# Chunk-selected attention with a gated feed-forward: the order of all work drawn anew, without a dependence of the weight transfers on the first loads

## The chip, the cores and the metric

The kernel runs on one core of one Trainium2 chip. The metric is device microseconds of the whole execution; lower is better. The core has five engines with a queue of instructions each, worked off in order: TensorE (PE), VectorE (DVE), ScalarE (ACT), GpSimd (POOL) and SyncE (SP). Transfers are issued by SyncE (all loads of q, k and v, the stores, and transposing copies inside the chip) and by GpSimd (the weights, which are turned from 32 to 16 bits on the way).

## The reference

```
k_min, k_max = min, max of k over chunks of 32 keys
ub  = sum_d max(q*k_min, q*k_max)          # a bound for each query and chunk, causal chunks only
sel = the 6 chunks with the largest ub, for each query
scores = q k^T / 8, kept where sel and causal; attn = softmax(scores); a = attn v
x   = a with the heads side by side         # 4*768 = 3072 rows of 8*64 = 512
out = (sigmoid(x w_gate) * (x w_val)) w_out # 512 -> 1536 -> 512
```

q, k and v have 4 batches, 8 heads, 768 positions and 64 columns; everything comes and goes in 32 bits.

## The kernel before

The 24 blocks of 128 queries are grouped in eight units of three blocks. Unit 0 holds the first blocks of batches 0, 1 and 2, where no choice of chunks is needed; its short way is the function `first` (names with `f`: `scf`, `expf`, `cmf`, `pvf`, `xf`, `xpsf`, `xTf`, with the batch as the number). Units 1 and 2 hold the rest of batch 0 (and the first block of batch 3); units 3 to 7 the rest of batches 1 to 3.

A unit goes through these steps. q and k are turned so that the head's columns lie across the partitions (`qn`/`kn` copy, `qT`/`kT` turn on TensorE, `qf`, `kt`, `hk`, `hq` copy back; from unit 3 on VectorE turns them itself: `k16`, `kt`, `qf0`). `kx0`, `kx1`, `kcr` take the chunks' minima and ranges, `qm` the positive part of q, `ub` the bounds on TensorE, and `ubn`, `mx`, `ap`, `apt`, `hqm` the choice, which is added to the scores as extra rows of the product. `sc` are the scores, `exp` the exponentials, `cm` the causal edge, `pv` the product with the values (`v16`), `rz` and `x` the division, `xps`/`xT` the turn back (from unit 3 on a transposing transfer on SyncE). Then the feed-forward: `g` and `v` are the gate's and the value's product for one of twelve blocks of 128 columns (`v_u0_2`: unit 0, block 2; `vb`, `gb` the third block of rows of the first four), `tanh` the gate, `hg` their product, `o0` to `o2` the output's product, `osb` and `out` the copy and the store. Units 4 with 5 and 6 with 7 share a faster product (`P`, `E`, `C`, `S`, `T`, `Q`, `F`, `G`).

Loads: `k0_u1` to `q3_u2` bring a pair of heads' k or q for unit 1 (192 KB) or unit 2 (128 KB); `kf0_1`, `qf1_2` and the like bring half the heads of a batch's first block (128 KB); `vf_1` brings that block's values (256 KB); `v_0_3` the values of a later block; `k01_3` and the like a quarter of a batch's k (384 KB). There are 31 loads ahead of the first `v_0_*`. The weights come in nine pieces, `wg0` to `wg2`, `wv0` to `wv2`, `wo0` to `wo2`; pieces 0 serve the blocks 0 to 3 of the feed-forward, pieces 1 the blocks 4 to 7, pieces 2 the blocks 8 to 11.

Nothing chooses at run time. Each step is an `Op` with its reads, writes and possible engines; `ORDER` is a written-out list of all of them, with the engine where it is not the first possible one (`@DVE`) and the numbers of the buffers that are taken (`:5,0,1`). `Plan.order` reads it, and the instructions are issued to their engines in this order. Semaphores follow from reads and writes of data; the dependences that `Op` records beyond that serve whoever draws up the list.

The weights' functions are these; `after` is a copy of one element of a loaded tile:

```python
def after(key, part, prio):
    plan.add(f"after{prio}", {POOL: (110, 150)}, lambda e: nc.gpsimd.tensor_copy(word[0:1, prio:prio + 1], ...),
             reads=[key], writes=[f"after{prio}"], prio=-2.0)

def weights(i, prio, after):
    lo, hi = 512 * i, 512 * i + 512
    return plan.add(f"wg{i}", {POOL: (760, 760)}, lambda e: nc.gpsimd.dma_start(wg16[:, :, lo:hi], wgs[:, :, lo:hi]),
             reads=after, writes=[("wg", i)], prio=prio, ...
```

`after0` to `after3` read the tiles of unit 1's q loads, `after4` to `after6` those of `vf_0`, `vf_1` and `vf_2`. `beat0`, `beat1`, ... are fillers: `BEATS[i]` turns of the unit matrix on TensorE whose result nobody reads. In the order before, GpSimd has these instructions ahead of the feed-forward's start:

```
ident epat v11 after3 tri hkq001 qn_u2_3 qn_u1_0 after0 hkq000 hkq100 hk1_u1_1 after1 hq0_u1_1 vf1_1 hq0_u1_3 v10 after4
hkq101 after2 vf1_3 hkf1 after6 vf1_2 after5 wv0 hk0_u1_2 wg0 wg1 wv1 wg2 hk1_u1_2 wv2 hq1_u1_2 hq1_u1_1 kn_u2_0 wo0
```

Of the kernel before, what the change touches and what calls it, by code (L numbers as in the profile page):

```python
# [97 lines left out]
ident q3_u1:0 epat0:0 k0_u1 tri0 ap1 epat q2_u1 k1_u1 q3_u2:1 q1_u1 q0_u1 kn_u1_0:0 qn_u1_3@DVE:1 ap0 v11 kf1_0:0
after3 beat0:7 kT_u1_0:0 tri kcr0 k3_u1 hkq011 qn_u1_2@DVE:2 kf0_0 hkq001@POOL hq0 kt_u1_0:0 qT_u1_2:1 qf1_0:1
hkp001@ACT hk0_u1_0 k2_u1 kx0_u1_0 qn_u2_3@POOL:0 qf0_0 kn_u1_1@DVE:2 hkp011@ACT qn_u1_1@DVE:3 vf_0:2 beat1:7  # L100
qT_u1_1:2 qn_u1_0@POOL:4 kT_u1_1:3 hk1_u1_0@ACT after0 hkq000@POOL qT_u1_0:4 kx0_u1_1 hkq100@POOL kn_u1_3:4 kf0_1:3
kx1_u1_0:0 kt_u1_1:0 beat2:7 kT_u1_3:5 kx1_u1_1 kfT_0:0 hk1_u1_1@POOL qf_u1_1@DVE:0 q0_u2 kt_u1_3:1 qT_u2_3:3 after1
qT_u1_3:6 kxf1:1 kf1_1 hk1_u1_3@ACT hq0_u1_1@POOL k2_u2 qf_u1_2 vf1_1:1 kn_u1_2@DVE:0 beat3:7 qfT_0:2 qf_u1_3 qf0_1:0
kxf0 kT_u1_2:1 hq0_u1_3@POOL qf1_1 qf16_0:4 v10 qm_u1_2@ACT:0 vf_1:0 hk0_u1_1 qf_u1_0 after4 qf_u2_3@DVE:1 kf16_0:0
kcr_f kx0_u1_3 hkq101@POOL vf_2:1 beat4:7 scf_0:0,4,1 after2 vf1_3:2 kfT_1:3 expf_0_1:2 kn_u2_2@DVE:4 expf_0_0 hkf1
kx0_u1_2 beat5:7 kT_u2_2:4 qf0_2:3 kx1_u1_3 kf16_1:3 q2_u2 ident16 qm_u1_3@ACT beat6:7 qfT_1:0 cmf_0_0@DVE qf1_2
v16_0_0@ACT cmf_0_1@DVE kx1_u1_2 qf16_1:4 kf1_2:0 beat7:7 pvf_0_0:3 hq0_u1_0 rzf_0_0:0 k1_u2 beat8:7 scf_1:0,5,1
xf_0_0:0 kx1_u2_2:1 kf0_2 expf_1_0 xpsf_0_0:3,0 kt_u1_2@DVE:0 k3_u2 after6 expf_1_1:3 vf1_2:3 hk0_u1_3 k0_u2
qm_u1_0@ACT after5 vc_1@DVE wv0 qm_u1_1@ACT kx0_u2_2 q1_u2 hq1_u2_3 hk0_u1_2@POOL v_0_3:2 hkf0@ACT beat9:7 qfT_2:5 wg0
cmf_1_0@DVE pvf_0_1:1 v_0_2:1 xTf_0_0@ACT qn_u2_2@DVE:0 qf16_2@DVE:4 kn_u2_1:5 wg1 beat10:7 qT_u2_2:3 pvf_1_0:0  # L110
cmf_1_1@DVE beat11:7 kfT_2:5 kcr_u1 wv1 rzf_1_0:0 xf_1_0:0 kf16_2:0 rzf_0_1:1 wg2 hkq010 kn_u2_3:6 xf_0_1:1 beat12:7
scf_2:5,0,1 pvf_1_1:2 hk1_u1_2@POOL ub_u1:1,6 expf_2_1:2 rzf_1_1:1 wv2 xf_1_1:2 expf_2_0 cmf_2_1@DVE vc_2@ACT
cmf_2_0@DVE xpsf_1_1:5 xpsf_1_0:2 kT_u2_1:0 hq1_u1_2@POOL ubn1_u1:0 qf_u2_2 pvf_2_0:7 v_0_1:0 qm_u2_2@ACT:0 xpsf_0_1:3
hq1_u1_1@POOL rzf_2_0:1 pvf_2_1:6 xTf_1_0@ACT kx0_u2_1 kt_u2_2:0 kn_u2_0@POOL:3 xf_2_0:1 beat13:2 kT_u2_3:2 qn_u2_1:5
rzf_2_1:0 wo0 xTf_1_1@ACT xpsf_2_0:7 xf_2_1:0 kt_u2_1:1 qn_u2_0@DVE:6 beat14:4 xpsf_2_1:6 xTf_0_1@ACT ubn0_u1
qT_u2_1:5 hq0_u1_2@POOL xTf_2_0@ACT qT_u2_0:4 kx0_u2_3 xTf_2_1@ACT v_u0_2:1 hkp111@POOL kx1_u2_3 hkp000@ACT vb_u0_2
kt_u2_3@DVE:2 v_u0_1:6 ubm0_u1 mx0_u1:0 hk0_u2_3@POOL vb_u0_1 hkp010@ACT v_u0_0:2 wo1 vb_u0_0 ap0_u1 v_u0_3:7
qm_u2_3@POOL apt0_u1:0 qf_u2_0 vb_u0_3 kx1_u2_1 qf_u2_1 hqm0_u1_0@ACT ubm1_u1 hkp100 beat15:3 g_u0_0:0,0,0 mx1_u1
hk1_u2_3@POOL gb_u0_0 hk0_u2_1@POOL g_u0_3:5,1,1 hqm0_u1_2 tanh_u0_0 gb_u0_3 k00_1:1 sc_u1_0_2:4,0 hg_u0_0 sc_u1_0_1:0
wo2 tanh_u0_3 g_u0_1:3,2,2 exp_u1_0_1 gb_u0_1 hg_u0_3 g_u0_2:5,0,3 qm_u2_0@ACT hk0_u2_2 tanh_u0_1 gb_u0_2 qm_u2_1  # L120
sc_u1_1_0:7,2 hq0_u2_2@POOL exp_u1_0_2 hg_u0_1 sc_u1_0_0:3 exp_u1_1_0 hq0_u2_1@POOL sc_u1_1_2:0 sc_u1_2_2:4,1
g_u0_6:2,1,4 hkq111 tanh_u0_2 ap1_u1 exp_u1_1_2 sc_u1_2_1:7 hq1_u2_1@POOL g_u0_7:5,2,5 exp_u1_0_0 exp_u1_2_1 kT_u2_0:0
sc_u1_3_1:3,3 tanh_u0_7 g_u0_5:6,3,6 kx0_u2_0 tanh_u0_6 kx1_u2_0 sc_u1_2_0:5 hq1_u1_3@DVE tanh_u0_5 kcr_u2@POOL
kt_u2_0@DVE:2 exp_u1_3_1 v16_0_3@DVE hq1 apt1_u1 hg_u0_2 g_u0_4:7,0,7 sc_u1_3_2:6 v_u0_6:0 v_u0_7:3 hqm1_u1_0 v_u0_4:2
tanh_u0_4 hg_u0_7 hq1_u1_0@POOL exp_u1_2_2 v_u0_5:7 exp_u1_2_0 hg_u0_4 hq1_u2_2 ub_u2:4,3 cm_u1_2@DVE exp_u1_3_2
hg_u0_5 hkq110@ACT sc_u1_3_0:7 ubn1_u2:0 g_u0_10:6,3,8 exp_u1_3_0 hqm1_u1_2@DVE g_u0_11:3,0,9 hg_u0_6 ubn0_u2
g_u0_8:0,1,10 mx0_u2:0 sc_u1_1_1:4 g_u0_9:7,2,11 exp_u1_1_1 ap0_u2 v16_0_2@DVE v_u0_8:4 tanh_u0_9 kcr1 apt0_u2:0
tanh_u0_10 v_u0_11:7 cm_u1_3@DVE hqm0_u2_2@ACT cm_u1_0@DVE v_u0_10:6 tanh_u0_8 v16_0_1 v_u0_9:2 tanh_u0_11 hg_u0_10
hk1_u2_2@POOL hqm0_u2_0@ACT pv_u1_2:3 hg_u0_11 cm_u1_1 sc_u1_5_0:6,1 sc_u1_5_2:7 hg_u0_9 pv_u1_3 exp_u1_5_0 pv_u1_1:0
hg_u0_8 sc_u1_5_1:2 sc_u1_6_2:6,3 cm_u1_5 rz_u1_1:0 pv_u1_0 x_u1_1:0 exp_u1_6_2 sc_u1_6_0:4 hq0_u2_0@POOL o0_u0_0:5,1  # L130
exp_u1_5_1 exp_u1_6_0 sc_u1_4_2:2,0 sc_u1_6_1:3 cm_u1_6@DVE k01_1 sc_u1_7_1:4,2 exp_u1_4_2 sc_u1_7_0:6 rz_u1_0:0
sc_u1_4_0:1 x_u1_0:1 o0_u0_1:2,0 exp_u1_7_0 exp_u1_7_1 cm_u1_7@DVE o1_u0_1 exp_u1_5_2 mx1_u2 hk0_u2_0@ACT exp_u1_6_1
ap1_u2 sc_u1_4_1:7 sc_u1_7_2:4 o1_u0_0 apt1_u2 exp_u1_4_1 hqm1_u2_0@DVE exp_u1_7_2 exp_u1_4_0 xps_u1_1:7,0 pv_u1_5:4
xT_u1_1 pv_u1_7:3 hq1_u2_0 hqm1_u2_2@DVE pv_u1_6 sc_u2_1_0:7,2 hkp110 sc_u2_1_1:1 sc_u2_7_0:6,3 cm_u1_4 rz_u1_3:0
k10_1 sc_u2_7_2:0 x_u1_3:0 o2_u0_0 exp_u2_7_0 hk1_u2_1@POOL hkp101@POOL exp_u2_1_0 sc_u2_0_0:6,1 exp_u2_7_2
sc_u2_0_1:3 osb_u0_0@DVE pv_u1_4 exp_u2_0_0 hk1_u2_0@POOL xps_u1_3:0 sc_u2_6_1:5,0 rz_u1_2:0 k11_1 xps_u1_0:7
exp_u2_0_1 x_u1_2:0 o2_u0_1 xT_u1_0 xT_u1_3 sc_u2_7_1:7 sc_u2_6_0:0 osb_u0_1@DVE xps_u1_2:3 exp_u2_7_1 xT_u1_2
exp_u2_6_0 qf1_3:0 exp_u2_6_1 out_u0_0 o0_u0_2:4,1 sc_u2_1_2:3 o1_u0_2 hq0_u2_3 v_0_4:1 exp_u2_1_1 o2_u0_2 v_0_5:2
k16_1_2@ACT:3 k16_1_1@DVE:6 k16_1_0:5 g_u1_4:1,1,4 kx1_1_2:1 v_1_1:3 exp_u2_1_2 g_u1_0:5,2,8 cm_u2_1 cm_u2_0 osb_u0_2
kt_1_0:1 v_u1_3:3 cm_u2_7 q11_1:0 sc_u2_6_2:4 g_u1_3:0,0,9 kx0_1_1 hk0_1_0 exp_u2_6_2 v_u1_4:7 tanh_u1_3 kx1_1_3  # L140
cm_u2_6 tanh_u1_0 v_u1_2:4 v16_0_4 tanh_u1_4 kt_1_1:5 k16_1_3:0 sc_u2_0_2:5 v16_0_5@ACT v_u1_0:0 v_u1_7:1 hk0_1_1@ACT
kf1_3:2 hg_u1_0 out_u0_1 pv_u2_6:2 hg_u1_4 sc_u2_4_0:0,0 qf0_3 kx0_1_0 pv_u2_7 exp_u2_4_0 sc_u2_2_0:7,3 kf0_3
g_u1_2:6,1,10 exp_u2_0_2 rz_u2_3:0 q01_1 x_u2_3:0 v16_1_1@ACT v_u1_9:0 cm_u2_4@DVE kx1_1_0 tanh_u1_2 xps_u2_3:2,1
g_u1_7:5,2,11 exp_u2_2_0 kx0_1_2 xT_u2_3@ACT g_u1_9:6,3,5 tanh_u1_7 pv_u2_1:2 q00_1 hg_u1_7 tanh_u1_9 sc_u2_2_2:5
g_u1_11:7,2,6 hg_u1_2 hg_u1_3 sc_u2_3_2:4,2 v_u1_11:6 exp_u2_3_2 kx1_1_1 tanh_u1_11 qfT_3:3 q10_1 sc_u2_3_0:4 hg_u1_11
sc_u2_4_2:7 g_u1_10:1,0,7 hg_u1_9 v_u1_10:6 kt_1_3:6 tanh_u1_10 exp_u2_3_0 sc_u2_2_1:0 vf_3:0 pv_u2_0 hg_u1_10
exp_u2_2_1 g_u1_8:1,3,0 cm_u2_3 kx0_1_3 exp_u2_2_2 cm_u2_2 sc_u2_4_1:0 kfT_3:6 tanh_u1_8 rz_u2_0:0 k01_2:1 kcr_1@POOL
kt_1_2:0 qf16_3:4 sc_u2_5_0:5,1 v_u1_1:1 exp_u2_4_1 x_u2_0:0 g_u1_5:3,0,1 exp_u2_5_0 qf0_u3_0:1 kf16_3:3 sc_u2_5_1:2
hk1_1_0@DVE sc_u2_3_1:5 k11_2 v_u1_5:0 vc_3 qf0_u3_1 exp_u2_3_1 qf0_u3_2 sc_u2_5_2:6 exp_u2_4_2 v_u1_6:5 qf0_u3_3
exp_u2_5_1 xps_u2_0:7 cm_u2_5@DVE v_u1_8:4 tanh_u1_5 qm_u3_0@POOL:0 qf0_u4_2:0 k00_2 qm_u3_2@ACT hg_u1_5 pv_u2_3:3  # L150
pv_u2_2 exp_u2_5_2 xT_u2_0 qf0_u4_1 g_u1_6:7,0,2 hg_u1_8 hk1_1_1 scf_3:6,0,3 rz_u2_1:0 pv_u2_4:4 x_u2_1:0 expf_3_0
k10_2 pv_u2_5 g_u1_1:3,3,3 expf_3_1:0 cmf_3_0@DVE rz_u2_2:0 ub_u3:6,2 cmf_3_1 qf0_u4_3 tanh_u1_1 x_u2_2:1 tanh_u1_6
hq1_u3_0@POOL hg_u1_1 hk1_1_3@ACT v_1_2:0 hg_u1_6 pvf_3_1:7 pvf_3_0:1 hk1_1_2 xps_u2_1:4 o0_u1_0:3,0 rzf_3_1:0
out_u0_2 xf_3_1:0 rzf_3_0:1 hk0_1_2 v_2_1:2 ubn0_u3:0 o1_u1_0 qf0_u4_0 ubm0_u3 k16_2_0@ACT:0 xf_3_0:2 k16_2_3:2
q01_2:0 o2_u1_0 xT_u2_1 mx0_u3:0 k16_2_2@ACT:5 hq0_u3_2@POOL xpsf_3_1:4 o0_u1_1:1,1 ubn1_u3 ap0_u3 xps_u2_2:2 ubm1_u3
# [1253 lines left out]
```

## Time and profile before

| | us |
|---|---|
| median of 3 runs | 282.54 (280.86 to 287.28) |
| profiled execution, its own time | 282.25 |
| its span, first to last instruction | 280.2 |
| TensorE busy | 268.8 (96%) |
| VectorE busy | 246.8 (88%) |
| ScalarE busy | 220.4 (79%) |
| GpSimd busy | 134.6 (48%) |
| read from memory, written | 30.67 MB, 6.29 MB |

A row of a group gives busy time and the mean of one instruction; a row in order of time gives the start, the duration and, in brackets, the idle time ahead of it with what ended it. In a table by stage the columns are the stretch, its length, busy time with the count for PE, PEld (the weights' load into the array), DVE, ACT and POOL, then the granted clock, the busy share of the DMA engines and GB/s. L968 is the line of `g` and `v`, L876 of `sc`, L480 of the fillers, L359, L361 and L365 of copies on ScalarE, VectorE and GpSimd, L528, L529 and L534 of the weights, L936 of the transposing transfer, L573 of the quarters of k and q, L583 of `v_*`.

### The profile page before, as it was taken

How to read it: one execution, taken by the hardware profiler on the slowest of the kernel's cores; microseconds unless marked ns; L12 is line 12 of the kernel's file. 1: busy time of each engine (PE TensorE's matmuls, PEld its weight loads, DVE VectorE, ACT ScalarE, POOL GpSimd, SP SyncE). 2: the span in 40 equal slices, each digit the busy share in tenths (PEclk: the TensorE clock that was granted, in tenths of full speed). 3: DMA queues.
4: the chain of work that ended last, by engine and by line, in shares of the span. 5: the costliest groups of instructions: out<-in, count | busy, mean ns of one | idle time of the engine just before them, and what ended most of it. 6: DMA issues, size and time to landing. Idle time of an engine off the chain costs nothing.

```text
span 280.2 us, 7449 instructions
## 1 busy us (share of the span) xinstructions
PE 268.8 (96%) x2758; PEld 186.3 (67%) x2758; DVE 246.8 (88%) x679; ACT 220.4 (79%) x474; POOL 134.6 (48%) x206
## 2 busy tenths in 40 slices
...
GB/s 187 261 225 186 197 195 205 165 186 159 209 167 201 203 214 167 140 196 169 214 170 155 27 14 45 91 1 54 0 18 44 0 100 82 2 37 0 4 37 225
DMA packets 131699, 34.68 MB, mean 124 GB/s; under 512 B 119760, under 2 KB 128720, under 8 KB 131664
## 3 DMA queue, kind: packets, MB, share of 16 engines
...
q0 software_dynamic: 4752, 4.72, 10.2%
...
HBM read 30.67 MB, written 6.29 MB: 132 GB/s over the span
## 4 chain that ended last, share of the span: by engine, by line
PE 83%; DVE 5%; ACT 4%; DMA 3%; issue 2%; SPq 1%; POOL 0%; ACTq 0%; DVEq 0%
PE sc_u L876 12%; PE g_u L968 11%; PE v_u L968 10%; PE o_u L1006 10%; PE pv_u L912 6%; PE suo_u6u L1233 3%; PE suo_u4u L1233 3%; PE sug_u4u L1092 3%; PE suv_u4u L1092 3%; PE sug_u6u L1092 2%; PE suv_u6u L1092 2%; PE ube_u L814 2%; DMA k<-in_k_dram 2%; DMA kq_u<-in_q_dram 1%; PE sro_u4u L1233 1%
## 5 line engine op out<-in xcount | busy, mean ns | idle before, releaser
L887 ACT ACTIVATE att_u<-sc_u 128x512 f16<-128x512 f32 (+3 forms) x184 | 90.9, 549 | 15.1 <-PE sc_u L876 12.7
L896 POOL TENSOR_SCALAR_AFFINE_SELECT att_u<-att_u 128x384 f16<-128x384 f16 (+1 forms) x48 | 26.8, 570 | 44.0 <-ACT att_u L887 42.8
L968 PE MATMUL g_u<-xT_u,wg 128*128 128x384 f16 (+2 forms) x208 | 37.6, 314 | 0.0
L968 PE MATMUL v_u<-xT_u,wv 128*128 128x384 f16 (+2 forms) x208 | 36.4, 313 | 0.0
L1006 PE MATMUL o_u<-wo,hg_u 128*128 128x512 f16 x144 | 35.3, 379 | 0.1
L876 PE MATMUL sc_u<-hqe,hke 128*128 128x128 f16 (+2 forms) x220 | 28.2, 243 | 1.6 <-ACT hqe L359 1.2
L987 DVE SCALAR_TENSOR_TENSOR hg_u<-gate_u,v_u 128x384 f16<-128x384 f16 x48 | 24.8, 538 | 4.7 <-PE v_u L968 3.1
L912 PEld LDWEIGHTS <-att_u 128*128 128x128 f16 x640 | 25.0, 98 | 5.0 <-issue 1.2
L876 PE MATMUL sc_u<-hqo,hko 128*128 128x128 f16 (+2 forms) x220 | 27.9, 243 | 0.0
L912 PE MATMUL pv_u<-v,att_u 128*128 128x65 f16 x640 | 27.0, 193 | 0.0
L982 ACT ACTIVATE gate_u<-g_u 128x384 f16<-128x384 f32 x48 | 22.7, 498 | 5.0 <-PE g_u L968 3.3
L968 PEld LDWEIGHTS <-wv 128*128 128x128 f16 x208 | 19.1, 98 | 10.1 <-issue 0.5
L968 PEld LDWEIGHTS <-wg 128*128 128x128 f16 x208 | 18.9, 98 | 9.5 <-issue 0.2
L876 PEld LDWEIGHTS <-hke 128*128 128x128 f16 x220 | 16.6, 98 | 8.9 <-issue 1.9
L1006 PEld LDWEIGHTS <-hg_u 128*128 128x128 f16 x144 | 13.2, 98 | 11.9 <-issue 0.7
L876 PEld LDWEIGHTS <-hko 128*128 128x128 f16 x220 | 17.0, 98 | 5.8
L931 DVE TENSOR_TENSOR x_u<-pv_u,rz_u 128x384 f16<-128x384 f32 (+1 forms) x28 | 15.0, 534 | 1.2 <-DMA xT_u<-x_u 0.4
L365 POOL CAST v<-v 128x512 f16<-128x512 f32 x15 | 9.1, 612 | 12.9 <-DMA v<-in_v_dram 9.4
L480 PE MATMUL beat<-ident 128*128 128x128 f32 x70 | 12.0, 305 | 1.4 <-POOL ident masks.py:199 1.4
L837 DVE MAX8 mx_u<-ubn_u 128x8 f32<-128x8 f32 (+16 forms) x152 | 12.7, 159 | 0.1
L1092 PEld LDWEIGHTS <-Sg 128*128 128x128 f16 x96 | 9.0, 98 | 5.2
L1092 PEld LDWEIGHTS <-Sv 128*128 128x128 f16 x96 | 9.0, 98 | 5.0 <-issue 0.3
...
## 6 DMA issues: line engine op xcount, KB each, us to landing
v<-in_v_dram SPq DMA_DIRECT2D x23, 256.0 KB, 4.5
...
out_dram<-osb_u SPq DMA_DIRECT2D x16, 256.0 KB, 2.5
wv<-in_moe_w_val_dram POOLq DMA_DIRECT2D x3, 512.0 KB, 14.8
wg<-in_moe_w_gate_dram POOLq DMA_DIRECT2D x3, 512.0 KB, 12.3
...
out_dram<-osb_u6u SPq DMA_DIRECT2D x5, 256.0 KB, 2.0
```

Of the source, the lines that this page charges most:

```text
L837: nc.vector.max(at(mx)[:, e_, j, :], at(ubn)[:, e_, j, 0:max(8, u.seen[j])])
L876: nc.tensor.matmul(at(t)[:, o:o + 128 * m], hk[b % 2][e_][:, p, 128 * jb:128 * jb + 128], hq[u.side][e_][:, p, 128 * x:128 * (x + m)], sta ...
L887: plan.add(f"exp_{u.name}_{h}_{y}", {ACT: act(n)}, lambda e, t=t, att=att, b0=b0, n=n: nc.scalar.activation(at(att)[:, b0:b0 + n], at(t), ...
L896: nc.gpsimd.affine_select(out=dv, in_=dv, compare_op=ALU.is_ge, fill=0.0, base=0, pattern=[[0, u.m], [1, 128]], channel_multiplier=-1)
L912: nc.tensor.matmul(at(pv)[:, last, x, :], at(att)[:, c:c + 128], v16[b % 2][:, jb, h, :], start=(jb == 0), stop=(jb == ib))
L931: plan.add(f"x_{u.name}_{p}", {DVE: dve(u.t)}, lambda e: nc.vector.tensor_tensor(at(x_).rearrange("p a (e d) -> p e a d", e=2), at(pv)[:, ...
L968: nc.tensor.matmul(at(t)[:, lo:hi], w16[:, c, 128 * fb:128 * fb + 128], at(u.xt)[:, c, lo:hi], start=(c == 0), stop=(c == 3))
L982: plan.add(f"tanh_{u.name}_{fb}", {ACT: act(T)}, lambda e, g=g, gate=gate: nc.scalar.activation(at(gate), at(g), AF.Tanh, scale=0.5), read ...
L987: plan.add(f"hg_{u.name}_{fb}", {DVE: dve(T)}, lambda e, w_=w_, gate=gate, hg=hg: nc.vector.scalar_tensor_tensor(at(hg), at(gate), 1.0, at ...
L1006: nc.tensor.matmul(at(o), hgs[c][1][1]()[:, 128 * tb:128 * tb + 128], wo16[:, fc, lo:hi], start=(c == 0), stop=(c == NFB - 1))
L1092: nc.tensor.matmul(at(t), left[i](c), right[i](c), start=first and c == 0, stop=c == 1, skip_group_check=not first)
L1233: nc.tensor.matmul(at(t), sums[what[i][0], f][1]()[:, 128 * tb:128 * tb + 128], what[i][1](f), start=first and f == 0, stop=f == half - 1, ...
```

## The change

The weights are added without the list of `after` copies. The copies themselves stay. The whole order is drawn anew: the list has 1998 words instead of 1999 (one filler less), 163 steps have another engine, and the buffers are numbered anew.

```diff
-BEATS = (14, 9, 4, 3, 8, 1, 3, 2, 1, 10, 2, 1, 4, 2, 2, 4)
+BEATS = (17, 3, 5, 1, 8, 1, 6, 3, 5, 2, 3, 2, 1, 4, 1)
...
-    weights(0, -0.9, late)
+    weights(0, -0.9, [])
     for i in range(1, 3):
-        weights(i, -0.5 + 0.2 * i, late)
+        weights(i, -0.5 + 0.2 * i, [])
     for i in range(3):
-        weights_out(i, 0.3, late)
+        weights_out(i, 0.3, [])
```

GpSimd's own list in the new order, up to the last weight piece:

```
ident epat kn_u1_1 qn_u1_0 hkq000 vf1_2 wv0 hq0_u1_0 hkq100 hk0_u1_0 qn_u1_1 vf1_3 v10 kn_u1_2 hkq010 kn_u1_3 vf1_1 after2
tri qn_u2_0 qn_u2_1 v11 hk0_u1_3 qn_u2_2 cmf_0_0 wg0 wg1 wv1 hk1_u1_2 cmf_1_0 wg2 cmf_2_1 hq1_u2_3 after5 after6 wv2 hkf1
after3 hk1_u1_3 hq1_u1_3 hkq111 hk0_u1_1 hkf0 hqm0_u1_2 hq1_u1_0 wo0 hk0_u2_0 wo1 hkq110 wo2
```

SyncE's first loads, in the old and in the new order:

```
old  q3_u1 k0_u1 q2_u1 k1_u1 q3_u2 q1_u1 q0_u1 kf1_0 k3_u1 kf0_0 qf1_0 k2_u1 qf0_0 vf_0 kf0_1 q0_u2
     kf1_1 k2_u2 qf0_1 qf1_1 vf_1 vf_2 qf0_2 q2_u2 qf1_2 kf1_2 k1_u2 kf0_2 k3_u2 k0_u2 q1_u2
new  q1_u1 k1_u1 q0_u1 k0_u1 q3_u2 kf0_0 k2_u1 q2_u1 kf1_0 q3_u1 k3_u1 q0_u2 qf0_0 qf1_0 qf0_1 qf1_2
     q1_u2 q2_u2 kf1_1 kf0_1 qf1_1 qf0_2 vf_0 kf1_2 kf0_2 k0_u2 vf_2 vf_1 k2_u2 k1_u2 k3_u2
```

TensorE's new list ahead of the first `v_u0`, fillers left out:

```
qT_u1_0 kT_u1_1 kT_u1_0 kfT_0 qT_u2_3 qT_u1_1 kT_u1_2 qT_u1_2 qT_u1_3 kT_u1_3 qfT_0 qT_u2_0 qT_u2_1 scf_0 kfT_1 qfT_1
qT_u2_2 qfT_2 scf_1 pvf_0_0 pvf_0_1 kfT_2 ub_u1 xpsf_0_1 xpsf_0_0 scf_2 pvf_1_1 kT_u2_0 pvf_1_0 pvf_2_0 xpsf_1_1 kT_u2_2
xpsf_1_0 pvf_2_1 xpsf_2_0
```

Around the last k the order of SyncE is, old: `k11_3 k00_3 v_2_3 xT_u3_0 v_2_0 k10_3 xT_u3_1 v_1_5 v_2_2 k01_3`, and new: `k11_3 k00_3 xT_u3_0 v_2_2 out_u1_2 k01_3 k10_3 xT_u3_1`. The casts `k16_3_3` and `k16_3_2` are ScalarE's and GpSimd's in the old order, both GpSimd's in the new one.

374 lines of the change are left out of this document (187 added, 187 removed).

## The prediction

> **What bounds the kernel now.** I read the page first, then the busy time by stage, the chain that ended last, GpSimd's and SyncE's instructions in order of time, and the waits of one stretch. Two per cent, 5.7 us, is about what a measurement of this kernel can tell from no change.
>
> ```profile
> span 280.2 us, 7449 instructions
> PE 268.8 (96%) x2758; PEld 186.3 (67%) x2758; DVE 246.8 (88%) x679; ACT 220.4 (79%) x474; POOL 134.6 (48%) x206
> GB/s 187 261 225 186 197 195 205 165 186 159 209 167 201 203 214 167 140 196 169 214 170 155 27 14 45 91 1 54 0 18 44 0 100 82 2 37 0 4 37 225
> ...
> 0.00:10.00 10.00, 7.31 (x43) 6.28 (x43) 5.96 (x15) 5.46 (x8) 6.48 (x17) 1.00 0.79 212
> 10.00:20.00 10.00, 8.54 (x81) 7.01 (x82) 8.72 (x24) 8.97 (x20) 4.79 (x16) 1.00 1.02 239
> 20.00:30.00 10.00, 8.13 (x109) 5.59 (x108) 8.60 (x26) 8.44 (x21) 8.63 (x14) 1.00 1.11 189
> 30.00:40.00 10.00, 10.00 (x102) 8.03 (x100) 8.36 (x41) 8.48 (x20) 6.18 (x12) 1.00 1.22 196
> 120.00:140.00 20.00, 18.35 (x184) 10.94 (x183) 17.64 (x54) 15.35 (x31) 10.84 (x18) 1.00 0.94 191
> ...
> 29.36 2.71 PE v_u L968 x32
> ```
>
> TensorE is busy 96% of the span, and from the first feed-forward matmuls (v_u0, at 29.36 us) it hardly stops: 30 to 40 shows 10.00 of 10.00, and only 120 to 140 lacks 1.65 us. So the kernel is a start of 29.36 us, then a stream bound by TensorE, then the last store. The same matmuls stand behind v_u0 in both orders, apart from fillers: a start that is late by x is late by x at the end, unless a stall later in the stream disappears. The start is also full on another resource: the next to last column, the busy share of the 16 DMA engines, reads 0.79, 1.02 and 1.11 in the first three rows.
>
> **Which transfers share those engines.** Bytes per issue, from the page, and GpSimd's weight issues with the times to landing:
>
> ```profile
> kf<-in_k_dram SPq DMA_DIRECT2D x8, 128.0 KB, 3.5
> qf<-in_q_dram SPq DMA_DIRECT2D x8, 128.0 KB, 3.3
> vf<-in_v_dram SPq DMA_DIRECT2D x4, 256.0 KB, 4.1
> kq_u<-in_q_dram SPq DMA_DIRECT2D x4, 192.0 KB, 3.7
> kq_u<-in_k_dram SPq DMA_DIRECT2D x4, 192.0 KB, 4.0
> kq_u<-in_q_dram SPq DMA_DIRECT2D x4, 128.0 KB, 3.7
> kq_u<-in_k_dram SPq DMA_DIRECT2D x4, 128.0 KB, 3.7
> q0 software_dynamic: 4752, 4.72, 10.2%
> ...
> 19.14 1.05 POOL L529 DMA_DIRECT2D wv<-in_moe_w_val_dram  x1 [0.37 <-issue]
> 20.84 1.49 POOL L528 DMA_DIRECT2D wg<-in_moe_w_gate_dram  x2
> 22.32 0.76 POOL L529 DMA_DIRECT2D wv<-in_moe_w_val_dram  x1
> 24.34 0.74 POOL L529 DMA_DIRECT2D wv<-in_moe_w_val_dram  x1
> DMA to landing us min/median/max: 7.4/14.8/19.5
> DMA to landing us min/median/max: 9.3/12.3/17.5
> ```
>
> The last two rows are for wv and wg. The 31 loads ahead of the stream are 8 of 192 KB, 8 of 128 KB (units 1 and 2), 12 of 128 KB (kf and qf of three batches) and 3 of 256 KB (vf): 4864 KB, 4.98 MB. The first three slices of 7.0 us moved 1.31 + 1.83 + 1.58 = 4.72 MB, so they are nearly through at 21 us. The first weight piece is issued at 19.14. The old gate thus lets the weights in when some 0.3 MB of first loads are left. Landings: wv0 at 19.14 + 7.4 = 26.5, wg0 at 20.84 + 9.3 = 30.1, wv1 at 22.3 + 14.8 = 37.1, wv2 at 24.34 + 19.5 = 43.8. One queue delivers a piece of 512 KB every 3.4 us, that is 154 GB/s.
>
> ```profile
> 30.00:45.00 15.00, 15.00 (x160) 10.81 (x158) 12.52 (x50) 11.74 (x27) 7.39 (x14) 1.00 1.22 197
> 21.24 9.14 SPq L583 DMA_DIRECT2D v<-in_v_dram  x3
> 47.75 0.61 POOL L365 CAST v<-v 128x512 f16<-128x512 f32 x1 [6.02 <-DMA v<-in_v_dram]
> ```
>
> This is the row on which the forecast rests. While weights flow, all transfers together make 197 GB/s, so SyncE's queue gets 197 - 154 = 43 GB/s, a sixth of the 261 it had alone. Three v loads (0.79 MB) issued from 21.24 on are so slow that GpSimd still waits for one at 47.7. In this kernel nothing needs them sooner.
>
> **The change, part by part.**
>
> ```profile
> 5.15 0.55 DVE L361 COPY qn_u<-kq_u 128x384 f32<-128x384 f32 x1 [0.47 <-DMA kq_u<-in_q_dram]
> 8.07 0.50 POOL L365 COPY qn_u<-kq_u 128x384 f32<-128x384 f32 x1 [0.93 <-DMA kq_u<-in_q_dram]
> ```
>
> (1) The dependence of the weights on `after0` to `after6` binds only whoever draws up the order: on the chip GpSimd held the weights because all seven copies stood ahead of wv0 in its own queue. They stay in the order, at other places. On an engine that is busy 48% they cost nothing by themselves. wv0 becomes GpSimd's seventh instruction, behind qn_u1_0 (which needs the third load), hkq000 and a memset. In the rows just shown the third load's reader starts at 5.15 us and a copy takes 0.50; with two copies and the memset wv0 issues near 6.4. I let it move from about 8.2 to 11.7. In these 3.4 us the first loads get 0.15 MB at 43 GB/s, where alone they had 261 x 3.4 = 0.89 MB. The bounds are thus 0 (sharing without loss) and 0.74 MB, 3 us; I take 0.5 MB, 2.2 us, since it is the larger pieces that move here.
>
> (2) wg0, wg1 and wv1 stand behind cmf_0_0, which moves from VectorE to GpSimd. scf_0 now follows qT_u2_1, and that needs the 17th load (2.75 MB). With part 1's loss it lands near 15.7; then five short instructions of 0.4 to 0.6 us (copy, transposes, scf_0, exp, cmf_0_0): wg0 issues at 18.4 to 19.2 and moves from 20.2. By then the first loads have 1.31 + 1.83 + 6.2 x 0.225 - 0.5 = 4.0 MB, exactly through the 26th of 31. Still to come are vf_2, vf_1 (27th, 28th; they were 22nd and 21st) and k2_u2 (29th; it was 18th): 640 KB, 0.66 MB. And wg2 follows at about 22.5, so four pieces stand in the queue, 4 x 3.4 = 13.6 us.
>
> At 43 GB/s the 0.66 MB take 15 us; after 13.6 us the weights are through and the rest is quick. vf_1 and k2_u2 land at about 34. TensorE runs in order: xpsf_1_0 (from vf_1) and kT_u2_2 (from k2_u2) stand ahead of v_u0_0. Cast, pvf, reciprocal, product, turn and copy are another 2.0 us: v_u0 starts near **36.0 instead of 29.36, +6.6 us**. What hid the weights before, 4.7 MB already landed, is gone. Bounds: ScalarE has 37 instructions instead of 45 ahead of v_u0 and VectorE 54 instead of 61; by the first three stages' busy time (22.9 us for 49 instructions, 23.3 for 65) that is 3.7 and 2.5 us less, so -2.7 if DMA never binds; +8.6 if the loads end at 36.
>
> after5 and after6 now stand ahead of wv2 and wait for vf_1 and vf_2, with hkf1, hk1_u1_3 and wo0 behind them on GpSimd. wv2 lands about 40, needed only after eight blocks, some 10 us into the stream: nothing.
>
> (3) Five fillers fewer ahead of v_u0 (62 against 67): below 0.7 us and inside waits. But TensorE now waits for several us:
>
> ```profile
> 1.42 3.25 PE L480 MATMUL beat<-ident 128*128 128x128 f32 x14 [1.42 <-POOL ident masks.py:199]
> 12.92 1.04 PE L480 MATMUL beat<-ident 128*128 128x128 f32 x8
> ```
>
> The first burst takes 0.23 us a filler, a later one 0.13. If the wait brings the slow rate back, 3.25 us run at half speed: 0 to +1.6, I take +0.8. [...]
>
> (4) The order behind v_u0:
>
> ```profile
> 113.09 4.18 SPq L936 DMA_TRANSPOSE xT_u<-x_u  x1
> ...
> 118.57 5.43 DMA k<-in_k_dram
> ...
> ACT k L359 <- DMA k<-in_k_dram: 3.0, 1, 3.0
> PE sc_u L876 <- ACT hqe L359: 1.2, 1, 1.2
> ```
>
> Now SyncE holds k01_3 behind xT_u3_1 (4.18 us), ScalarE waits 3.0 us for it in k16_3_3, and TensorE stalls behind hqm0_u4. In the new order both last pieces of k_3 precede xT_u3_1, and the first two casts are GpSimd's. Gain 0 to 3.0; I take -2.0.
>
> (5) 163 instructions change engine (ScalarE gains five, VectorE loses four, GpSimd one): nothing as a sum. New tight places: ub_u2 to the first sc_u2 is 6.8 us of matmuls instead of 14, xT_u3_3 leaves 3.2 us to the first g_u3 where a transposing DMA takes
>
> ```profile
> xT_u<-x_u SPq DMA_TRANSPOSE x12, 3.3
> ```
>
> from its issue. Bounds: -1 (the stream's other gaps are short), +3.0 (one stall like that of ScalarE); I take +1.0.
>
> Sum: 6.6 + 0.8 - 2.0 + 1.0 = +6.4 us on the profiled execution's 282.25 (2.05 more than its span, and 0.3 below the median 282.54): **288.7 us**.
>
> **Rivals.** *Faster, the gate was the cost.* FFN could start when 4.7 MB and wv0 have landed; with wv0 early and less work ahead on ScalarE and VectorE, v_u0 starts 2.7 us sooner and wg0, at 3.4 us less of queue, keeps up: 282.25 - 2.7 - 2.0 + 1.0 = 278.6. For it: the margins of the weights now are only 2 to 3 us (wv0 lands 26.5, used 29.36). Against: 43 GB/s. It decides by when wg0 issues: every us later lets 0.23 MB through alone, worth 5 us of starved transfer; from an issue at 21.5 on nothing is starved. Chance 0.17.
>
> *The change does not do what it says.* Eight of nine pieces still stand behind instructions that wait for first loads, as by the old gate; if cmf_0_0 comes 1.5 to 2 us later than I reckon, only wv0 has moved: 2.2 us from part 1, less fillers and k_3: 282.25 + 2.2 - 2.0 + 1.0 = 283.5. Chance 0.25.
>
> *The gain goes elsewhere.* No starvation, but both tight places of part 5 stall: 282.25 + 2 x 3.0 = 288.2. Against: both distances hold the chain by the old durations. Chance 0.08.
>
> **Numbers.** The forecast's own chance is 0.50, with v_u0 at 33 to 38 it spans 285 to 292. Range 279.5 to 293.5: it takes in the faster rival and leaves 0.2 outside. Slower by over 2% (above 288.2): 0.40 from the forecast, 0.03 from the last rival, 0.05 from the second with a new stall: 0.48. Faster by over 2% (below 276.9): 0.09, half of the first rival. Within: 0.43.
>
> **What would show it.** Right: wv issued before 8 us, wg before 20; vf_1's cast and kn_u2_2 start after 31 and wait for DMA; v_u0 after 33 with TensorE idle for 5 us or more between 22 and 36; no ScalarE wait of 3 us for k near 120. Wrong: v_u0 before 31, or loads that keep over 100 GB/s beside the weights, or an end later than v_u0's delay explains.

## The result, and the profile after

The changed kernel takes 291.45 us (median of 4 runs, 288.01 to 291.95) where the kernel before, measured with it, takes 282.59 (4 runs): a ratio of 1.031, with a 95% interval from 1.0264 to 1.0355. It is slower. Ratios, here and in the table of experiments, leave out executions over 1.5% above their kernel's fastest, which the medians keep; a2's ratio alone does not come out by this rule, and its two medians give 1.041. The traced execution is the shortest of the four, 288.01 us with a span of 286.3, so its trace shows 5.8 of the 8.9 us; where the others lose some 3.5 us more had to be found by experiment. First the rows of its page that answer to those of before, and the table by stage (columns as before):

```profile
span 286.3 us, 7410 instructions
PE 270.8 (95%) x2750; PEld 188.4 (66%) x2750; DVE 247.9 (87%) x675; ACT 224.7 (79%) x479; POOL 130.5 (46%) x205
...
0.00:10.00 10.00, 7.70 (x35) 7.19 (x36) 2.39 (x5) 4.17 (x6) 7.11 (x16) 1.00 0.80 217
10.00:20.00 10.00, 7.25 (x63) 6.14 (x62) 9.32 (x24) 8.11 (x14) 4.05 (x14) 1.00 0.93 189
20.00:30.00 10.00, 6.11 (x89) 4.52 (x90) 6.13 (x17) 6.55 (x14) 6.82 (x13) 1.00 1.11 206
30.00:40.00 10.00, 9.37 (x101) 8.03 (x100) 8.79 (x36) 7.42 (x18) 6.20 (x13) 0.83 1.21 204
120.00:140.00 20.00, 20.00 (x203) 12.05 (x201) 17.81 (x84) 18.55 (x36) 14.40 (x22) 1.00 0.88 173
200.00:220.00 20.00, 18.97 (x198) 12.56 (x197) 19.76 (x40) 18.52 (x44) 12.88 (x16) 1.00 0.10 20
```

TensorE loses 1.3 us against before in 10 to 20 (7.25 against 8.54), 2.0 in 20 to 30 (6.11 against 8.13) and 0.6 in 30 to 40, where its granted clock is 0.83; it wins back 1.65 in 120 to 140. In the second row the loads run at 189 GB/s instead of 239, and VectorE has done only 2.39 us of work by 10 us where it had done 5.96. The next rows, in order of time, tell the start: SyncE's loads, GpSimd's weights, and who waits.

```profile
7.02 4.19 SPq L552 DMA_DIRECT2D qf<-in_q_dram  x4
18.14 0.37 SPq L547 DMA_DIRECT2D vf<-in_v_dram  x1
20.28 1.29 SPq L547 DMA_DIRECT2D vf<-in_v_dram  x2
21.61 4.06 SPq L563 DMA_DIRECT2D kq_u<-in_k_dram  x3
...
6.91 0.92 POOL L529 DMA_DIRECT2D wv<-in_moe_w_val_dram  x1
21.44 1.53 POOL L528 DMA_DIRECT2D wg<-in_moe_w_gate_dram  x2
29.44 0.43 DVE L361 CAST vf<-vf 128x512 f16<-128x512 f32 x1 [3.53 <-DMA vf<-in_v_dram]
29.92 0.29 PE L678 MATMUL pvf<-vf,attf 128*128 128x65 f16 x4 [3.60 <-DVE vf L361]
31.56 0.41 ACT L359 COPY kn_u<-kq_u 128x256 f32<-128x256 f32 x1 [4.05 <-DMA kq_u<-in_k_dram]
33.48 1.06 PE L968 MATMUL v_u<-xT_u,wv 128*128 128x256 f16 x4
39.06 0.74 POOL L534 DMA_DIRECT2D wo<-in_moe_w_out_dram  x1
DMA to landing us min/median/max: 3.0/4.3/8.6
```

`vf_2` and `vf_1` are sent at 20.28, against 13.02 before, and one of them lands 8.6 us later (the last row is for `vf`), beside the weights of 21.44. VectorE waits 3.53 us for it, TensorE 3.60 us for VectorE; ScalarE waits 4.05 us for a piece of unit 2's k. `v_u0` starts at 33.48 instead of 29.36, 4.1 us late. Behind it the stream takes 286.3 - 33.5 = 252.8 us instead of 250.8.

### The profile page after: what moved, and what is told of

The parts are those of the page before. It is cut to its first block, busy times and chain, and to the rows that moved or that the text cites. A ratio compares the mean times of both kernels' runs of the same rounds, so it can differ in the third digit from the quotient of the medians.

```text
span 286.3 us, 7410 instructions
## 1 busy us (share of the span) xinstructions
PE 270.8 (95%) x2750; PEld 188.4 (66%) x2750; DVE 247.9 (87%) x675; ACT 224.7 (79%) x479; POOL 130.5 (46%) x205
## 4 chain that ended last, share of the span: by engine, by line
PE 71%; DVE 10%; ACT 6%; DMA 6%; issue 4%; SPq 2%; POOL 0%; DVEq 0%; ACTq 0%
PE v_u L968 11%; PE g_u L968 10%; PE sc_u L876 10%; PE o_u L1006 8%; PE pv_u L912 5%; DMA vf<-in_v_dram 3%; ACT att_u L887 3%; PE suo_u6u L1233 3%; PE suo_u4u L1233 3%; PE ube_u L814 3%; PE suv_u6u L1092 2%; PE sug_u6u L1092 2%; ACT gate_u4u L1117 2%; PE sro_u4u L1233 1%; PE sro_u6u L1233 1%
## 5 line engine op out<-in xcount | busy, mean ns | idle before, releaser
L887 ACT ACTIVATE att_u<-sc_u 128x512 f16<-128x512 f32 (+3 forms) x184 | 91.9, 553 | 12.6 <-PE sc_u L876 9.1
L896 POOL TENSOR_SCALAR_AFFINE_SELECT att_u<-att_u 128x384 f16<-128x384 f16 (+1 forms) x45 | 23.9, 534 | 49.8 <-ACT att_u L887 49.4
L968 PE MATMUL g_u<-xT_u,wg 128*128 128x384 f16 (+2 forms) x208 | 38.3, 314 | 0.7 <-ACT att_u L887 0.6
L968 PE MATMUL v_u<-xT_u,wv 128*128 128x384 f16 (+2 forms) x208 | 38.0, 317 | 0.0
L987 DVE SCALAR_TENSOR_TENSOR hg_u<-gate_u,v_u 128x384 f16<-128x384 f16 x48 | 25.5, 540 | 8.3 <-PE v_u L968 6.6
L876 PE MATMUL sc_u<-hqo,hko 128*128 128x128 f16 (+2 forms) x220 | 28.8, 243 | 0.5 <-DVE hg_u L1122 0.4
L982 ACT ACTIVATE gate_u<-g_u 128x384 f16<-128x384 f32 x48 | 23.3, 502 | 3.2 <-PE g_u L968 2.1
L876 PEld LDWEIGHTS <-hke 128*128 128x128 f16 x220 | 17.2, 98 | 8.1 <-issue 0.8
L1215 POOL TENSOR_TENSOR v<-v,hg_u 128x384 f16<-128x384 f16 x5 | 5.0, 1006 | 17.5 <-DVE hg_u L1122 14.4
L365 POOL CAST k<-k 128x768 f16<-128x768 f32 x9 | 7.3, 828 | 10.5 <-DMA k<-in_k_dram 9.9
```

Source lines behind the costliest of these rows:

```text
L876: nc.tensor.matmul(at(t)[:, o:o + 128 * m], hk[b % 2][e_][:, p, 128 * jb:128 * jb + 128], hq[u.side][e_][:, p, 128 * x:128 * (x + m)], sta ...
L887: plan.add(f"exp_{u.name}_{h}_{y}", {ACT: act(n)}, lambda e, t=t, att=att, b0=b0, n=n: nc.scalar.activation(at(att)[:, b0:b0 + n], at(t), ...
L896: nc.gpsimd.affine_select(out=dv, in_=dv, compare_op=ALU.is_ge, fill=0.0, base=0, pattern=[[0, u.m], [1, 128]], channel_multiplier=-1)
L968: nc.tensor.matmul(at(t)[:, lo:hi], w16[:, c, 128 * fb:128 * fb + 128], at(u.xt)[:, c, lo:hi], start=(c == 0), stop=(c == 3))
L982: plan.add(f"tanh_{u.name}_{fb}", {ACT: act(T)}, lambda e, g=g, gate=gate: nc.scalar.activation(at(gate), at(g), AF.Tanh, scale=0.5), read ...
L987: plan.add(f"hg_{u.name}_{fb}", {DVE: dve(T)}, lambda e, w_=w_, gate=gate, hg=hg: nc.vector.scalar_tensor_tensor(at(hg), at(gate), 1.0, at ...
```

## The experiments

Each edit moves words of `ORDER` or changes buffer numbers in it. The theory on record was starvation: weights that share the DMA engines with the first loads make these crawl. Its rivals were that the late loads are SyncE's own doing, and that the new order has a price of its own. The table gives the start of `v_u0` in the traced execution, the median, and the ratio to runs of the kernel before that were measured beside it. A piece is called gated where it waits on GpSimd's list behind `after5` and `after6`, that is for the values of batches 1 and 2.

| | edit | v_u0 | median, us | ratio (95%) |
|---|---|---|---|---|
| before | | 29.4 | 280.3 to 281.8 | |
| a2 | the changed kernel again | 33.9 | 292.26 | 1.043 (1.040 to 1.047) |
| w1 | wv0 late | 34.4 | 295.2 | 1.037 (1.028 to 1.045) |
| w2 | wg, wv1 gated | 31.0 | 287.21 | 1.018 (1.013 to 1.024) |
| w3 | both | 30.8 | 288.44 | 1.021 (1.015 to 1.027) |
| s1 | three loads early | 36.6 | 288.92 | 1.015 (1.006 to 1.025) |
| s2 | three buffer numbers | 31.5 | 291.34 | 1.036 (1.033 to 1.040) |
| x1 | wo late | 33.6 | 286.81 | 1.019 (1.014 to 1.024) |
| x2 | x1 and fillers | 32.6 | 288.88 | 1.027 (1.019 to 1.034) |
| x3 | x1, s2 and w2 | 30.4 | 285.13 | 1.015 (1.011 to 1.020) |
| x4 | x3, wg0 not gated | 29.6 | 283.03 | 1.013 (1.006 to 1.019) |
| b1 | before without its gate | 47.8 | 298.06 | 1.062 (1.057 to 1.067) |
| b2 | before, k01_3 earlier | 29.4 | 280.34 | 0.9973 (0.9949 to 0.9997) |

**w1, the early piece moved late.**

```diff
 GpSimd:
- ident epat kn_u1_1 qn_u1_0 hkq000 vf1_2 wv0 hq0_u1_0 ... cmf_0_0 wg0 wg1
+ ident epat kn_u1_1 qn_u1_0 hkq000 vf1_2 hq0_u1_0 ... cmf_0_0 wv0 wg0 wg1
```

> The changed kernel with wv0 moved on GpSimd's list from the 7th place to right ahead of wg0. Starvation (the record's step 1: wv0 takes 2.2 us from the first loads): the first loads gain about 2 us, v_u0 starts near 31.5 instead of 33.5, the time is 289 to 290 against 291.5. Late issue (SyncE itself sends vf_2 and vf_1 only at 20.3 us, because their forerunners in its queue wait for buffers): v_u0 stays within 1 us of 33.5 and the time within 1 us of 291.5, or v_u0 comes later, since a fifth piece now stands in the weights' queue beside vf_1.

SyncE's queue in w1, stage 10 to 20, and the wait that follows:

```profile
12.01 1.05 SPq L552 DMA_DIRECT2D qf<-in_q_dram  x2
17.56 0.37 SPq L547 DMA_DIRECT2D vf<-in_v_dram  x1
10.00:20.00 10.00, 6.92 (x60) 5.81 (x61) 9.36 (x23) 8.11 (x15) 3.77 (x13) 1.00 0.65 151
...
30.89 0.38 PE L678 MATMUL pvf<-vf,attf 128*128 128x65 f16 x4 [5.15 <-DVE vf L361]
```

and in the changed kernel the first of these steps, with the turn on TensorE that frees `vf_0`'s buffer (`vf_0` itself goes out at 18.14, shown above):

```profile
16.26 1.05 SPq L552 DMA_DIRECT2D qf<-in_q_dram  x2
17.51 0.60 PE L625 MATMUL qfT<-ident,qf 128*128 128x128 f32 x4
```

Without wv0 SyncE gets through the loads up to qf0_2 4.2 us sooner (2.5 us in w3 below, where that pair is issued at 13.72), so wv0 did slow them, by more than the record's 2.2 us. But then SyncE stands at `vf_0`, which takes the buffer that qfT_0 still reads: 17.56 against 18.14, so 0.6 us of the 4.2 arrive, and the engines' share falls to 0.65. Behind it the piece makes the crowd larger, and the wait for `vf_1` grows to 5.15 us. The traced execution is a long one (296.57), so the start is what counts here.

**w2 and w3, the other pieces gated again.**

```diff
 GpSimd, w2:
- ... cmf_0_0 wg0 wg1 wv1 hk1_u1_2 cmf_1_0 wg2 cmf_2_1 hq1_u2_3 after5 after6 wv2
+ ... cmf_0_0 hk1_u1_2 cmf_1_0 after5 after6 wg0 wg1 wv1 wg2 cmf_2_1 hq1_u2_3 wv2
 w3: the same, and wv0 as in w1
```

> The changed kernel with after5, after6 and then wg0, wg1, wv1, wg2 right behind cmf_1_0 on GpSimd's list: four pieces wait for the values of batches 1 and 2, wv0 stays early. Starvation: vf_1 lands about 4 us after its issue (25 to 26 instead of 29.4), v_u0 starts at 29.5 to 30.5, TensorE keeps its clock of 1.00 from 30 to 40, and the time is 286 to 288. Late issue, the weights being harmless: vf_1 lands after 28.5, v_u0 starts after 32.5, the time stays at 291 or goes up because the gate's product now waits for wg0.

> Both moves together: wv0 beside cmf_0_0 (issue near 21), the other four pieces behind the wait for vf_1 and vf_2. Starvation: v_u0 at 28 to 30 (2 us from wv0, 3.5 us from the four), unless wv0's own landing, some 4 to 5 us after its issue, comes to set it at 26 to 27; time 284 to 287. Late issue: v_u0 after 32.5, time 291 or more.

The rows of w2:

```profile
26.36 0.56 POOL L523 COPY word<-vf 1x1 f32<-1x1 f32 x2 [0.90 <-DMA vf<-in_v_dram]
26.86 1.52 POOL L528 DMA_DIRECT2D wg<-in_moe_w_gate_dram  x2
30.97 0.60 PE L968 MATMUL v_u<-xT_u,wv 128*128 128x256 f16 x4
35.49 0.83 PE L968 MATMUL g_u<-xT_u,wg 128*128 128x256 f16 x8 [2.28 <-DMA wg<-in_moe_w_gate_dram]
```

Without four pieces beside it the last value load is there by 26.4 instead of 29.4, and `v_u0` starts 2.5 us sooner. So those pieces do starve the loads. The price of the gate is in the last row: TensorE waits 2.28 us for wg0, issued at 26.9. w3, with wv0 late as well, has the same start (30.8): again wv0's place hardly counts.

**s1 and s2, are the loads merely sent too late?**

```diff
 SyncE, s1:
- ... kf1_1 kf0_1 qf1_1 qf0_2 vf_0 kf1_2 kf0_2 k0_u2 vf_2 vf_1 k2_u2 k1_u2
+ ... kf1_1 kf0_1 vf_2 vf_1 k2_u2 qf1_1 qf0_2 vf_0 kf1_2 kf0_2 k0_u2 k1_u2
 buffers, s2:
- qf1_2:0 ... vf_0:1 ... v_0_1:0
+ qf1_2:5 ... vf_0:0 ... v_0_1:1
```

> The changed kernel, weights untouched, with vf_2, vf_1 and k2_u2 moved on SyncE's list to right behind kf0_1, so that they are sent near 16 to 17 us instead of 20.3 to 22. Both starvation and late issue expect them to land ahead of wg0's traffic: v_u0 at 29.5 to 30.5 and 286 to 288. If v_u0 still starts after 32, it is neither: the start's chain over VectorE, ScalarE and GpSimd in its new order sets it.

> The changed kernel with three buffer numbers changed (qf1_2, vf_0, v_0_1), so that SyncE's loads no longer wait for buffers that kfT_0 and qfT_0 still read; weights and all orders untouched. Starvation of what is sent late: all 31 loads are sent by about 17 us and land before wg0 moves at 22; no load takes over 6 us, v_u0 starts at 28.5 to 30.5, the time is 285 to 287.5. If the loads' bandwidth beside wv0 sets the start (the record's step 1), or the new order's chain over the engines, v_u0 stays after 32 and the time at 290 or more.

s1, whose traced execution is its longest (293.28; the others 284.49 to 289.7):

```profile
29.45 1.08 PE L625 MATMUL kfT<-ident,kf 128*128 128x128 f32 x4 [3.96 <-DMA kf<-in_k_dram]
```

The three loads moved ahead are no longer late, but now batch 2's k stands last and is starved in their place. In this execution the loads sent last beside the weights pay; the reordering only changed which. The shorter executions were not traced, and the fastest, 284.49, is below every one of the changed kernel, so whether sending these loads early helps stays open. In s2 SyncE has no buffer to wait for, but its issues themselves now take long (first row below; the engines' share from 10 to 20 is 0.99, with wv0 among the loads), so `vf_2` and `vf_1` go out at 19.89, only 0.4 us sooner; they land within 7.2 us instead of 8.6, and `v_u0` starts 2.0 us sooner. Yet all four executions take 290.7 to 291.5. The trace shows why:

```profile
9.56 3.42 SPq L563 DMA_DIRECT2D kq_u<-in_q_dram  x2
24.47 12.10 SPq L583 DMA_DIRECT2D v<-in_v_dram  x3
53.41 0.61 POOL L365 CAST v<-v 128x512 f16<-128x512 f32 x1 [4.74 <-DMA v<-in_v_dram]
54.08 0.43 PE L912 MATMUL pv_u<-v,att_u 128*128 128x65 f16 x5 [4.07 <-POOL v L365]
DMA to landing us min/median/max: 2.9/4.6/26.9
```

A second starvation, in nobody's forecast: `v_0_1` to `v_0_3`, sent from 24.5 on, land up to 26.9 us after their issue, about when the last weight piece is through; GpSimd's cast waits 4.74 us, and TensorE 4.07 us at `pv_u1`, with a granted clock of 0.91 from 40 to 60. The long trace of w1 has the same stall. In the trace of the changed kernel the same cast was just in time, and TensorE did not wait. The first row is w1's, the others are the changed kernel's:

```profile
56.54 0.43 PE L912 MATMUL pv_u<-v,att_u 128*128 128x65 f16 x5 [3.79 <-POOL v L365]
...
50.63 0.62 POOL L365 CAST v<-v 128x512 f16<-128x512 f32 x1 [1.32 <-DMA v<-in_v_dram]
51.42 0.43 PE L912 MATMUL pv_u<-v,att_u 128*128 128x65 f16 x9
```

**a2, the changed kernel again, and x1, the wo pieces late.**

```diff
 GpSimd, x1:
- ... hq1_u1_0 wo0 hk0_u2_0 wo1 hkq110 wo2 ... v16_0_3
+ ... hq1_u1_0 hk0_u2_0 hkq110 ... v16_0_3 wo0 wo1 wo2
```

> The changed kernel once more, for a second trace of it and as the measure of the runs beside it. In the first trace the values v_0_1 to v_0_3, sent from 25.8 us beside the weights, come so late that GpSimd's cast has no margin (waits of 1.3 us for the transfer); if the executions of 291.5 us, 3.5 us longer than the traced one, are those in which TensorE waits for such a cast, a trace of about 291 shows a wait of 2 to 4 us ahead of a pv_u near 55 us. If the length comes from the granted clock alone, it shows the same waits as before and more slices under 1.00. If this execution takes 288 again, this stays open.

> The changed kernel with wo0, wo1, wo2 moved on GpSimd's list to behind v16_0_3, the first of its casts of batch 0's later values (issue near 45 instead of 39 to 41.5); the start is untouched. Second starvation (v_0_1 to v_0_3 crawl beside the weights until the last piece is through): the values land by 45, no pv_u waits for a cast near 54, the long executions disappear and the median falls from 291.5 to 287.5 to 288.5. If the two lengths of the changed kernel come from elsewhere, the median stays above 290.5. v_u0 stays at 33.5 by both.

The trace of a2 fell on its shortest execution again (287.22; the other five 290.94 to 293.36), with no wait at `pv_u1`; it settles nothing about the long ones. x1 does more. GpSimd's casts and pieces there:

```profile
44.89 0.61 POOL L365 CAST v<-v 128x512 f16<-128x512 f32 x1
45.44 2.26 POOL L534 DMA_DIRECT2D wo<-in_moe_w_out_dram  x3
49.22 0.61 POOL L365 CAST v<-v 128x512 f16<-128x512 f32 x1
```

Neither cast waits, the start is unchanged (33.6), and three of four executions take 286.2 to 287.4: the median falls by 5.45 us against a2. One still takes 291.25, and of x2's four below, with the wo pieces late as well, two take 290.24 and 295.42: 3 of 8 executions are over 290, against 8 of 10 of the changed kernel. The long trace of s1 has no wait for a cast at `pv_u1`; it has this one:

```profile
106.66 0.81 PE L968 MATMUL g_u<-xT_u,wg 128*128 128x384 f16 x4 [2.09 <-ACT att_u L887]
```

The changed kernel waits 0.61 us at the same place. The stall at `pv_u1` is thus shown for s2 and w1, and taking the wo pieces away makes long executions rarer; it is not their only cause, and a long execution of the changed kernel itself was never traced.

**x2, TensorE kept busy in its wait.**

```diff
-BEATS = (17, 3, 5, 1, 8, 1, 6, 3, 5, 2, 3, 2, 1, 4, 1)
+BEATS = (17, 3, 5, 1, 8, 1, 6, 3, 5, 2, 3, 2, 1, 27, 1)
 TensorE, besides x1:
- ... scf_2 pvf_1_1 kT_u2_0 pvf_1_0 beat13 pvf_2_0
+ ... scf_2 beat13 pvf_1_1 kT_u2_0 pvf_1_0 pvf_2_0
```

> As the run with the wo pieces late, and 27 fillers instead of 1 in beat13, moved to right ahead of pvf_1_1, so that TensorE turns the unit matrix during its wait for vf_1 (27 x 0.109 = 2.9 us of 3.4 to 3.6). The record's step 3 (the wait brings the slow rate back, 0 to 1.6 us): the granted clock from 30 to 40 reads 1.00 instead of 0.83, the first four v_u0 matmuls take 0.6 instead of 1.06 us, and the time is 0.5 to 1.2 us below that run. If the clock costs nothing in this place, since the other engines set the pace there, the time is within 0.4 us of it.

The group held four fillers before, not one as the expectation says. Stage 30 to 40:

```profile
30.00:40.00 10.00, 8.98 (x100) 7.20 (x101) 8.54 (x36) 8.35 (x20) 5.82 (x12) 1.00 1.21 203
```

The clock reads 1.00 and `v_u0` starts 1.0 us sooner than in x1 (32.6 against 33.6), but the spans are 285.3 and 285.7 and the two fastest executions 287.07 and 287.52 against 286.18 and 286.24. The slow rate is real, and what it costs at the end is within the scatter of these runs; the median, with the two long executions in it, is 2.1 us above x1's.

**x3 and x4, every meeting of weights and needed loads taken out.** x3 is x1 with the buffer numbers of s2 and the gate of w2; x4 puts wg0 alone back.

```diff
 GpSimd, x4 against x3:
- ... cmf_0_0 hk1_u1_2 cmf_1_0 after5 after6 wg0 wg1 wv1 wg2
+ ... cmf_0_0 wg0 hk1_u1_2 cmf_1_0 after5 after6 wg1 wv1 wg2
```

> The new order with all that lets weights meet needed loads taken out: the wo pieces late, SyncE's three buffer numbers changed as in s2, and wg0, wg1, wv1, wg2 behind the wait for vf_1 and vf_2. If starvation is the whole of the loss, v_u0 starts at 29 to 30, the gate's product waits under 2.5 us for wg0, and the time is 281 to 284. If the new order has a price of its own (chains of the start, new gaps of the stream), 284.5 to 287 remain with no wait for a transfer over 2.5 us on TensorE.

> As x3, but wg0 is back in its place of the changed kernel right behind cmf_0_0 (issue near 21), while wg1, wv1 and wg2 still wait for vf_1 and vf_2. If starvation grows with the number of pieces in the queue, one piece costs the last loads 1 us at most: v_u0 at 30 to 31.5, no wait for wg0, and 1 us less than x3 (283.5 to 285). If any piece beside the loads starves them as four do, v_u0 comes at 32 or later and the time is 286 or more.

x4's start and its stage 30 to 40:

```profile
29.61 0.60 PE L968 MATMUL v_u<-xT_u,wv 128*128 128x256 f16 x4
30.00:40.00 10.00, 9.82 (x103) 7.89 (x102) 9.22 (x35) 9.31 (x23) 6.03 (x13) 1.00 1.22 201
200.00:220.00 20.00, 18.87 (x185) 12.46 (x183) 19.89 (x40) 18.33 (x43) 11.36 (x14) 1.00 0.08 17
```

In x3 TensorE still waits 1.8 us for wg0. x4 removes that, and one piece issued just behind the last values (22.05 against 20.83) does no harm: `v_u0` starts at 29.6, as before the change, and the median is 283.03. From the changed kernel's 292.26 (a2) down to 283.03, 9.2 us went with the meetings of weights and needed loads, SyncE's waits for buffers among them; measured against the kernel before that ran beside each, it is 8.7 us. The rest, 2.7 us to the 280.29 of the kernel before, is by subtraction the new order's own: x4's stream behind `v_u0` takes 281.4 - 29.6 = 251.8 us. The changed kernel's loss in 200 to 220 is in it still, 18.87 of 20.00, with two waits of TensorE for VectorE of 0.35 and 0.65 us, where before has

```profile
200.00:220.00 20.00, 19.84 (x195) 13.59 (x194) 19.77 (x45) 19.29 (x45) 11.30 (x15) 1.00 0.11 22
```

What else makes up the rest was not tried.

**b1 and b2, single steps of the change in the old order.**

```diff
 GpSimd, b1:
- ... hkq101 after2 vf1_3 hkf1 after6 vf1_2 after5 wv0 hk0_u1_2 wg0 wg1 wv1 wg2
+ ... hkq101 after2 vf1_3 wv0 wg0 wg1 wv1 wg2 hkf1 after6 vf1_2 after5 hk0_u1_2
 SyncE, b2:
- k11_3 k00_3 v_2_3 xT_u3_0 v_2_0 k10_3 xT_u3_1 v_1_5 v_2_2 k01_3
+ k11_3 k00_3 v_2_3 xT_u3_0 v_2_0 k10_3 k01_3 xT_u3_1 v_1_5 v_2_2
```

> The kernel before with wv0, wg0, wg1, wv1, wg2 on GpSimd's list behind vf1_3, ahead of the copies that wait for vf_1 and vf_2: issues at 14.3 to 19 us instead of 19.1 to 23.8, all else in the old order. Starvation: some 1.4 MB of first loads are left; at 43 GB/s beside 17 us of weights kf_2 and the last of unit 2 land after 30, v_u0 starts at 33 to 36, the time is 286 to 289. If the weights harm the loads only through the new order's own delays, v_u0 stays within 1 us of 29.3 and the time at 282.

> The kernel before with k01_3 moved on SyncE's list from behind xT_u3_1, v_1_5, v_2_2 to right behind k10_3, and nothing else. By the record's step 4 ScalarE no longer waits 3.0 us in k16_3_3, TensorE is busy for 20.0 instead of 18.35 us from 120 to 140, and the time falls by 1.5 to 2.5 us, to 279.5 to 280.5. If the stall only hid another wait, 120 to 140 stays under 19 and the time within 0.7 us of before.

b1, then the stage of b2:

```profile
15.66 0.99 POOL L529 DMA_DIRECT2D wv<-in_moe_w_val_dram  x1
20.96 3.61 SPq L563 DMA_DIRECT2D kq_u<-in_k_dram  x1
31.48 1.08 PE L625 MATMUL qfT<-ident,qf 128*128 128x128 f32 x4 [10.00 <-DMA qf<-in_q_dram]
39.72 1.09 PE L625 MATMUL kfT<-ident,kf 128*128 128x128 f32 x4 [5.54 <-DMA kf<-in_k_dram]
...
20.00:30.00 10.00, 1.38 (x12) 1.15 (x12) 2.29 (x8) 2.97 (x7) 3.70 (x9) 0.71 1.22 201
30.00:40.00 10.00, 2.98 (x19) 2.62 (x20) 2.34 (x8) 0.41 (x1) 0.00 (x0) 0.50 1.21 223
...
120.00:140.00 20.00, 20.00 (x212) 12.48 (x210) 19.21 (x59) 16.97 (x34) 10.79 (x18) 1.00 0.92 188
```

In b1 weights issued 3.5 us sooner hold `v_u0` back by 18.4 us: the direction that starvation expected, several times its size (33 to 36). The DMA engines are full throughout (1.22, 1.21) while the others do little, and TensorE waits 10.0 us for one load of 128 KB and 5.54 us for another. SyncE's issues grow long as well, 3.61 us for one load (second row above) that took 0.51 in the old order, and later loads queue behind them; the byte count left that out. In b2 the stall of 120 to 140 is gone, as expected, but the time falls by only 0.27% (0.03 to 0.51%), some 0.8 us. b2 is the one version here that comes out ahead of both kernels, by less than 0.3%.

## Why the prediction came out as it did

The forecast was 288.7 us and slower; the traced execution gave 288.01, the median 291.45. The mechanism held, in place and direction, but errors of opposite sign lie in the number. That the traced execution came within 0.7 us of the forecast is luck: `v_u0` was put 2.5 us too late (36.0 against 33.48) and the stream behind it, with the clock, 2.2 us too short (0.2 us less than before, against 2.0 us more); what makes most executions longer than the traced one was not in the sum.

**(1) wv0 early, +2.2 us: mis-sized, about nothing at the end.** In the sum it stands only through the 0.5 MB that (2) takes off. It was issued at 6.91 as reckoned (6.4) and did slow the loads, by 2.5 to 4.2 us at qf0_2. What the step left out is the buffer that `vf_0` waits for until 17.5 us in any case; that wait covers all but 0.6 us.

**(2) The late pieces, v_u0 at 36.0: right in kind, too large.** Measured 33.48, +4.1 instead of +6.6. wg0 issued at 21.44 instead of 18.4 to 19.2. By the record's first rival nothing is starved from an issue at 21.5 on, and by its second, with `cmf_0_0` 1.5 to 2 us later than reckoned, only wv0 has moved; w2 shows 2.5 us of starvation at 21.44. All fail at the same step: the loads still to come were counted from bytes, while they depend on when SyncE sends them: it sent `vf_0` at 18.14, after its buffer's wait, and `vf_2` and `vf_1` from 20.28 to 21.57, at the very time of wg0.

**(3) The clock, +0.8: its size held, at its place.** The granted clock was 0.83 from 30 to 40 (0.50 from 31 to 34), the first four `v_u0` matmuls took 1.06 us (0.60 in w2), x2 won 1.0 us at `v_u0`. The fillers ahead of `v_u0` are 62 against 66, four fewer and not five, which changes nothing. The changed kernel shows the lower clock after a wait of 3.60 us, and b1 0.50 over 30 to 40, its wait of 10.00 us ending at 31.5. Shorter waits stand before it too: s2 has 0.84 from 30 to 40 after a wait of 2.35 us, and x4 0.83 from 10 to 20, with no wait above 1.44 us up to 20. So these traces give no length of wait from which the clock falls. At the end little of it was seen: x2 and x1 differ by 0.4 us in span.

**(4) The order of k_3, -2.0: right in kind, mis-sized.** The wait of 3.0 us is gone and 120 to 140 is full, yet b2 prices the step at 0.8 us. The traced execution of before, 282.25, is longer than its medians beside the experiments (280.29 to 281.76); probably a stall read in one trace was taken for a stall of every execution, but no second one of before was traced.

**(5) Tight places, +1.0.** Neither of the two named ones stalls in the trace. The cost came from others, among them TensorE's waits of 0.61 us at 101.58 and of 0.36 and 0.65 us in 200 to 220; with (4) the record had -1.0 for the stream, the traces have +2.0 (252.8 against 250.8), part of it the clock.

**What was missing.** The record quoted the three v loads that crawled until 47.75 and added that in this kernel nothing needs them sooner. It did not carry that row into the new order. There these loads are sent from 25.77 on instead of 21.24, while the weights' queue moves its last packets between 52 and 54 us as before, although wo0 was issued at 39.06 instead of 27.97; and unit 1's product needs the values at 51 us. With the wo pieces late the median is 5.45 us lower (x1), but x2's two long executions forbid to put all of that down to the values. It is probably the largest single error, and it is hidden in the one trace because the cast there was just in time.

Of the signs named in advance, wv before 8 us, `v_u0` after 33 and no wait for k near 120 came true; the wait for unit 2's k (31.56) too. wg before 20 and the cast of `vf_1` after 31 did not (21.44, 29.44), TensorE's idle time was 4.5 us instead of 5. "An end later than v_u0's delay explains" was named as a sign against the forecast, and it occurred.
